# Gram products of a delta-rule attention: one 64x64 product per head in place of two smaller ones, and eight narrow PSUM copies in place of two wide ones

## The chip, the cores and the metric

The kernel runs on one core of a Trainium2 chip. The metric is the device time of one execution in microseconds: the median of the runs of a kernel. One execution of each kernel is also recorded by the hardware profiler, and the profile and trace quoted here are of that execution. Engines are named as in the profile: PE is TensorE, PEld its weight loads, DVE is VectorE, ACT is ScalarE, POOL is GpSimd, SP is SyncE, which issues the DMAs.

## The reference

Attention by a delta rule over 32 heads (4 batches of 8), 768 steps, 48 dimensions a head, and then a dense layer with softplus over the 3072 tokens (384 to 2048 to 384), all in fp32:

```python
k_n = k / (np.linalg.norm(k, axis=-1, keepdims=True) + 1e-06)
for t in range(S):
    y[:, :, t] = np.einsum('bhd,bhde->bhe', q[:, :, t], state)
    v_old = np.einsum('bhde,bhd->bhe', state, kt)
    state = state + bt[:, :, :, None] * np.einsum('bhd,bhe->bhde', kt, vt - v_old)
...
h = x @ w_in
g = np.maximum(h, 0.0) + np.log1p(np.exp(-np.abs(h)))
return g @ w_out
```

## The kernel before

The 768 steps are cut into 12 chunks of C = 64. Inside a chunk the recurrence is solved as a triangular system: for each head the matrix K K^T of the chunk (64x64, here called its Gram) is formed, its strict lower triangle is scaled and I + L is inverted by halves of HB = 32: the two 32x32 diagonal blocks are inverted on VectorE (`invert`), and the block below the diagonal is joined by products on TensorE (`cross_a`, `cross_b`). So three of the four 32x32 blocks of a Gram are needed: both diagonal ones and the one below.

The 32 heads lie in 16 pairs; a pair fills 128 partitions with 64 steps each. The keys of a chunk lie transposed in `kts[s % 3]`: 48 dimensions on the partitions, the first head of a pair in one half of them and the second in the other. `quads` (L59) lists the 32 products of a chunk so that neighbours go through all four combinations of the half that is read (`dr[ab]`) and the half of PSUM that is written (`t`). Even and odd pairs go to two PSUM tiles `pas[0]`, `pas[1]`, each 128 x 8 x 64.

`gram(s)` (L120) makes the Gram of chunks 2 to 11. First 32 products of 32x32 put the upper diagonal block at columns HB to C of the lower-numbered rows `lo` (L127), then 32 products of 32x64 put the block below the diagonal and the lower diagonal block into rows `hi` (L131). Both diagonal blocks then lie in the same columns, and one copy of 128 partitions for each parity takes them to `LTD` (`copy_diagonals`, L113, the tile is named `work`); four copies of 32 partitions take the blocks below to `OFF` (`copy_below`, L118). Chunks 0 and 1 are made by `gram_diagonal` and `gram_below` (L140, L148), of their own.

Every fp32 product is two matmul records and two weight loads in the trace. The small products write to the PSUM pool `ps_a` (tiles `pa`), which has 4 buffers that are handed out in turn: a Gram takes two, then `k_state` (L294) two, the two halves of `p_half` (L304) one each, and so on.

The order of the work: the attention of a chunk and the dense layer of an earlier chunk are generators that the loop at L720 advances in turn by a counted rate. For even s, `chunk(s)` makes the Grams of chunks s + 2 and s + 3 at its end (L556, L559), so they come in pairs close to each other: (4, 5), (6, 7), (8, 9), (10, 11); chunk 2's is in the hand-ordered start and chunk 3's stands alone. After the second Gram of a pair come the next chunk's `k_state` and `p_half`. The dense layer's products are L465 (into `ph`, waiting for softplus on ScalarE L469 to L471 and VectorE L473 to L476) and L448 (into `po`). A scheduler sets the order of each engine's queue from this program; within a queue the engine works in order. In the first chunk the weights are also rounded by a chain on VectorE (L394 to L406) with copies on ScalarE (L384, L409).

Of the kernel before, what the change touches and what calls it, by code (L numbers as in the profile page):

```python
# [20 lines left out]
C = 64  # L21
HB = 32
NS = S // C
NP = B * H // 2
# [11 lines left out]
def deltanet_moe(ctx, tc, kT, qT, kN, kI, vN, beta, wts, out):  # L36
    nc = tc.nc
# [14 lines left out]
    tk = [slice(h * C, (h + 1) * C) for h in range(2)]  # L52
    lo = [slice(h * C, h * C + HB) for h in range(2)]
    hi = [slice(h * C + HB, (h + 1) * C) for h in range(2)]
    dr = [slice((1 - h) * C, (1 - h) * C + D) for h in range(2)]
# [3 lines left out]
    quads = [(i, e, 2 * i + e, ab, ab ^ e) for i in range(NP // 2) for e in range(2)  # L59
             for ab in range(2)]  # L60
# [12 lines left out]
    W, HF, ST, OFF, TT, LTD, LDS, NN, NV, X = {}, {}, {}, {}, {}, {}, {}, {}, {}, {}  # L73
# [28 lines left out]
    def parity(t):  # L102
        return t.rearrange("p (a e) c -> p e a c", e=2)
# [3 lines left out]

        LTD[u] = one.tile([P, 2 * NP, HB], F32, name="work")

    def copy_diagonals(s, pas, c0):  # L110
        u, j = divmod(s, 2)
        for e in range(2):
            nc.scalar.copy(parity(LTD[u][:, j * NP:(j + 1) * NP])[:, e], pas[e][:, :, c0:c0 + HB])  # L113

    def copy_below(s, pas):
        for e in range(2):
            for h in range(2):
                nc.scalar.copy(parity(OFF[s])[hi[h], e], pas[e][hi[h], :, 0:HB])  # L118

    def gram(s):  # L120
        if s not in OFF:
            OFF[s] = two.tile([P, NP, HB], F32, name="off", bufs=3)
        pas = [ps_a.tile([P, NP // 2, C], F32, name="pa") for e in range(2)]
        kt = kts[s % 3]
        for i, e, p, ab, t in quads:
            k = kt[dr[ab], p, :]
            nc.tensor.matmul(pas[e][lo[t], i, HB:C], k[:, 0:HB], k[:, 0:HB],  # L127
                             start=True, stop=True)
        for i, e, p, ab, t in quads:
            k = kt[dr[ab], p, :]  # L130
            nc.tensor.matmul(pas[e][hi[t], i, :], k[:, HB:C], k, start=True, stop=True)  # L131
        copy_diagonals(s, pas, HB)
        copy_below(s, pas)

    def gram_diagonal(s, pool, name):
        pas = [pool.tile([P, NP // 2, HB], F32, name=name) for e in range(2)]
        for half in (lo, hi):
            for i, e, p, ab, t in quads:
                k = kts[s % 3][dr[ab], p, half[0].start:half[0].stop]
                nc.tensor.matmul(pas[e][half[t], i, :], k, k, start=True, stop=True)  # L140
        copy_diagonals(s, pas, 0)

    def gram_below(s):
        OFF[s] = two.tile([P, NP, HB], F32, name="off", bufs=3)
# [370 lines left out]
    def chunk(s):  # L515
# [36 lines left out]
        if more:  # L552
            u = s // 2 + 1
            systems(u)
            load_k(s + 3)
            gram(s + 2)  # L556
            cols[u] = run(nm)
            yield
            gram(s + 3)  # L559
            yield  # L560
            background.append(invert(u, *cols[u]))
# [12 lines left out]
    with tc.manual_schedule(engines={ET.PE, ET.DVE, ET.Activation, ET.Pool}):  # L574
# [28 lines left out]
        for _ in range(5):  # L603
            next(nm)
        gram_diagonal(0, ps_a, "pa")
        gram_diagonal(1, ps_a, "pa")
        cols[0] = run(nm)
        iv = invert(0, *cols[0])
# [18 lines left out]
        run(iv)  # L627
        systems(1)
        gram(2)
        finish(0)  # L630
        nm = norms(1, kas[1])
# [148 lines left out]
```

## Time and profile before

| | before |
|---|---|
| runs, us | 671.69, 673.43, 679.93 (median 673.43) |
| the profiled execution | 672.51, its span 670.8 |
| mean granted TensorE clock | 0.971 |
| matmuls of L127 and L131 | 640 records each, 9.0 and 13.2 us busy |
| copies of L113 and L118 | 24 and 48, 7.9 and 17.5 us busy |

The span is the time from the first to the last instruction of the profiled execution. A row of a timeline gives the start, the time, the engine, the line, the operation with its tiles, the shape, how many instructions are merged, and in brackets how long the engine had been idle and what released it. A row by groups gives after the bar the busy us and the mean ns of one, and the idle time before them. "issue" is time in which an engine waited for nothing that the profile shows. The idle time of an engine that others do not wait for costs nothing.

### The profile page before, as it was taken

What the parts mean: (1) busy time and instruction counts of PE and PEld (TensorE: products, weight loads), DVE (VectorE), ACT (ScalarE), POOL (GpSimd) and SP (SyncE); (2) the same over time, 40 slices, a digit from 0 to 9 for tenths busy, and PEclk for the clock granted to TensorE, in tenths of its full rate; (3) what the DMA queues carried; (4) which work ended last, traced back from release to release, by engine and by line L of the source; (5) the groups of instructions that cost most, each with busy time, mean ns of one, the idle gap of its engine ahead of it and who ended that gap; (6) DMA issues with size and microseconds to landing.
All of it is one profiled execution on the core that took longest, in us unless ns stands there. A gap on an engine that the chain in (4) does not pass through costs nothing.

```text
span 670.8 us, 24090 instructions
## 1 busy us (share of the span) xinstructions
PE 612.4 (91%) x10736; PEld 571.7 (85%) x10736; DVE 451.9 (67%) x970; ACT 372.5 (56%) x687; POOL 30.5 (5%) x56
## 2 busy tenths in 40 slices
PE   4456968899888999989999999999999999999997
PEld 3455756579888999988999999998999998999997
DVE  4966498978555985556997558985539984544443
ACT  4334767879664447464456555555554546454433
POOL 3200010000000001000001000001000001000000
PEclk9998977899998999999999999997999998999999
DMA  9837286000140120140210322200302100200000
GB/s 232 271 98 207 64 262 150 0 25 4 52 108 26 48 61 26 50 108 27 70 38 28 81 78 71 61 25 21 90 4 71 38 24 5 60 25 13 2 23 23
DMA packets 35095, 44.80 MB, mean 67 GB/s; under 512 B 21776, under 2 KB 27184, under 8 KB 34992
## 3 DMA queue, kind: packets, MB, share of 16 engines
q1 hardware_dynamic: 34992, 43.27, 22.9%
q8 instruction: 84, 1.38, 0.9%
q14 instruction: 19, 0.16, 0.1%
HBM read 36.27 MB, written 4.72 MB: 61 GB/s over the span
## 4 chain that ended last, share of the span: by engine, by line
PE 77%; ACT 8%; DVE 7%; issue 5%; DMA 2%; POOL 1%; SPq 0%; ACTq 0%; DVEq 0%; POOLq 0%
PE ph L465 29%; PE po L448 27%; PE pa L345 4%; PE pa L304 3%; PE pa L330 2%; PE pa L318 2%; PE pa L284 2%; PE pa L131 2%; PE pa L294 2%; DMA big<-qT 1%; ACT tt L275 1%; PE pa L263 1%; PE pa L127 1%; DVE ex L406 1%; DVE ex L403 1%
## 5 line engine op out<-in xcount | busy, mean ns | idle before, releaser
L465 PE MATMUL ph<-x,w 128*128 128x256 f32 x1680 | 240.9, 294 | 2.2 <-DVE a L473 0.9
L465 PEld LDWEIGHTS ph<-x,w 128*128 128x128 f32 x1680 | 224.6, 192 | 10.1 <-DVE w L419 1.2
L448 PE MATMUL po<-w,gh 128*128 128x384 f32 x768 | 208.0, 357 | 3.7 <-DVE gh L479 2.4
L469 ACT ACTIVATE a<-ph 128x512 f32<-128x512 f32 x96 | 57.5, 599 | 171.7 <-PE ph L465 171.7
L448 PEld LDWEIGHTS po<-w,gh 128*128 128x128 f32 x768 | 135.0, 190 | 13.6 <-DVE gh L479 3.2
L473 DVE SCALAR_TENSOR_TENSOR a<-ph,a 128x512 f32<-128x512 f32 x88 | 60.5, 689 | 106.6 <-ACT a L471 106.2
L448 PE MATMUL po<-w,gl 128*128 128x384 f32 x352 | 119.2, 339 | 0.0
L448 PEld LDWEIGHTS po<-w,gl 128*128 128x128 f32 x352 | 66.3, 188 | 0.5 <-DVE gl L476 0.2
L476 DVE TENSOR_TENSOR gl<-a,gh 128x512 fp32r<-128x512 f32 x88 | 60.9, 692 | 2.9
L470 ACT ACTIVATE a<-a 128x512 f32<-128x512 f32 x96 | 60.9, 634 | 2.7
L471 ACT ACTIVATE a<-a 128x512 f32<-128x512 f32 x96 | 60.8, 634 | 2.3
L229 DVE TENSOR_TENSOR Z<-Z,work 128x84 f32<-128x84 f32 (+14 forms) x148 | 44.2, 306 | 2.8
L223 DVE TENSOR_TENSOR work<-Z,ltq 128x84 f32<-128x84 f32 (+14 forms) x148 | 44.2, 305 | 2.5
L475 DVE CAST gh<-a 128x512 fp32r<-128x512 f32 x88 | 37.7, 428 | 7.7 <-PE po L448 5.6
L311 DVE TENSOR_TENSOR big<-pa,maskP 64x512 f32<-64x512 f32 x44 | 30.2, 687 | 12.9 <-PE pa L304 12.4
L345 PEld LDWEIGHTS pa<-big 128*64 128x64 f32 x768 | 27.8, 150 | 10.9 <-ACT big L322 7.1
L345 PE MATMUL pa<-big 128*64 128x64 f32 x768 | 31.0, 238 | 6.7 <-ACT big L322 5.7
L322 ACT COPY big<-pa 64x384 f32<-64x384 f32 x46 | 21.7, 473 | 19.5 <-PE pa L318 18.7
L277 POOL MEMSET tt<- 32x512 f32 x24 | 13.1, 545 | 402.3 <-PE pa L263 224.9
L304 PE MATMUL pa<-big,kt 48*64 48x64 f32 x704 | 27.4, 229 | 3.4 <-issue 2.0
L304 PEld LDWEIGHTS pa<-big,kt 48*64 48x64 f32 x704 | 24.9, 144 | 4.0 <-issue 2.3
L333 ACT COPY big<-pa 48x384 f32<-48x384 f32 x44 | 20.9, 475 | 8.4 <-PE pa L330 7.9
(103 smaller groups left out, 645.1 us busy)
## 6 DMA issues: line engine op xcount, KB each, us to landing
w<-wts SPq DMA_DIRECT2D x16, 768.0 KB, 5.6
kt<-kT SPq DMA_DIRECT2D x24, 192.0 KB, 4.3
big<-qT SPq DMA_DIRECT2D x24, 192.0 KB, 4.1
nv<-vN SPq DMA_DIRECT2D x12, 384.0 KB, 4.2
ki<-kI SPq DMA_DIRECT2D x24, 192.0 KB, 3.6
out<-ex SPq DMA_DIRECT2D x24, 192.0 KB, 1.9
ka<-kN SPq DMA_DIRECT2D x8, 384.0 KB, 3.6
x<-x SPq DMA_DIRECT2D x66, 32.0 KB, 2.2
```

Source lines behind the costliest of these rows:

```text
L223: nc.vector.tensor_tensor(tmp[:, a:a + r, 0:j], Z[:, a + j + 1:a + n, a + j:a + j + 1].to_broadcast([P, r, j]), lq[:, a + j:a + j + 1, a:a ...
L229: nc.vector.tensor_tensor(z, z, tmp[:, a:a + r, 0:j], op=ALU.add)
L304: nc.tensor.matmul(pt[tk[ab], i, :], kts[s % 3][dr[ab], 8 * g + i, :], bv[dr[ab], ab, 8 * g + i, 0:C], start=True, stop=True)
L345: nc.tensor.matmul(py[tk[ab], i, :], big[:, at + C:at + 2 * C], big[:, at:at + C], start=True, stop=True)
L448: nc.tensor.matmul(po[:, h, 0:DM], g[b][:, f - f0, h * P:(h + 1) * P], weight(f, a, DM, DM), start=(f == 0 and i == 0), stop=end)
L465: nc.tensor.matmul(ph[:, f - f0], weight(f, a, k * P, P), xr[b][k], start=(c == 0), stop=(c == len(terms1) * NK - 1))
L469: nc.scalar.activation(a, ph, AF.Abs)
L470: nc.scalar.activation(a, a, AF.Exp, scale=-1.0)
L471: nc.scalar.activation(a, a, AF.Ln, bias=1.0)
L473: nc.vector.scalar_tensor_tensor(a, ph, 0.0, a, op0=ALU.max, op1=ALU.add)
L475: nc.vector.tensor_copy(g[0], a)
L476: softplus[0] = nc.vector.tensor_tensor(g[1], a, g[0], op=ALU.subtract)
```

## The change

The whole 64x64 Gram of a head is one product: 32 products of 64x64 replace 32 of 32x32 and 32 of 32x64. The upper diagonal block now lies in columns 0 to HB of the rows `lo` and the lower one in columns HB to C of the rows `hi`, so the diagonal blocks are copied by eight copies of 32 partitions (2 parities, 2 halves, 2 blocks; new L132), where two of 128 did it. The block above the diagonal is computed and not read. `copy_diagonals` keeps its use in `gram_diagonal` alone. Lines below L131 move by one: L158 is now L159, L248 is L249, L294 is L295, L304 is L305, L448 is L449, L465 is L466, L469 is L470.

```diff
     def copy_diagonals(s, pas):
         u, j = divmod(s, 2)
         for e in range(2):
-            nc.scalar.copy(parity(LTD[u][:, j * NP:(j + 1) * NP])[:, e], pas[e][:, :, c0:c0 + HB])
+            nc.scalar.copy(parity(LTD[u][:, j * NP:(j + 1) * NP])[:, e], pas[e][:, :, 0:HB])
...
         for i, e, p, ab, t in quads:
             k = kt[dr[ab], p, :]
-            nc.tensor.matmul(pas[e][lo[t], i, HB:C], k[:, 0:HB], k[:, 0:HB],
-                             start=True, stop=True)
-        for i, e, p, ab, t in quads:
-            k = kt[dr[ab], p, :]
-            nc.tensor.matmul(pas[e][hi[t], i, :], k[:, HB:C], k, start=True, stop=True)
-        copy_diagonals(s, pas, HB)
+            nc.tensor.matmul(pas[e][tk[t], i, :], k, k, start=True, stop=True)
+        u, j = divmod(s, 2)
+        for e in range(2):
+            for h in range(2):
+                for rows, c in ((lo[h], 0), (hi[h], HB)):
+                    nc.scalar.copy(parity(LTD[u][rows, j * NP:(j + 1) * NP])[:, e],
+                                   pas[e][rows, :, c:c + HB])
         copy_below(s, pas)
```

The scheduler also orders the queues anew. ScalarE in the start, from the copies of chunk 2's Gram to the copy in the first `join` (L248, now L249); `x_84` and `ka` are natural-layout keys that are squared for the norms. Before:

```order
L113 COPY work<-pa 128x8x32 x2
L118 COPY off<-pa 32x8x32 x4
L158 ACTIVATE x_84<-x_84 128x768
L158 ACTIVATE ka<-ka 128x768
L248 COPY x_303<-pa 128x16x16
```

Changed:

```order
L132 COPY work<-pa 32x8x32 x4
L159 ACTIVATE ka<-ka 128x768
L132 COPY work<-pa 32x8x32 x4
L118 COPY off<-pa 32x8x32 x4
L159 ACTIVATE x_84<-x_84 128x768
L249 COPY x_303<-pa 128x16x16
```

The square of `ka` moved from behind the copies into the middle of them.

TensorE at the second Gram of the pair (8, 9), from chunk 9's Gram on. Before:

```order
L127 MATMUL pa<-kt_74 32x32 x32
L131 MATMUL pa<-kt_74 32x64 x32
L294 MATMUL pa<-big,kt_75 64x48 x32
L304 MATMUL pa<-big,kt_75 64x64 x16
L465 MATMUL ph<-x_5514,w_1765 128x256 x9
L465 MATMUL ph<-x_5514,w_1770 128x256 x9
L448 MATMUL po<-w_2624,gh 128x384 x2
L448 MATMUL po<-w_2624,gl 128x384
```

Changed:

```order
L127 MATMUL pa<-kt_74 64x64 x32
L295 MATMUL pa<-big,kt_75 64x48 x32
L466 MATMUL ph<-x_5358,w_1713 128x256 x9
L466 MATMUL ph<-x_5358,w_1718 128x256 x9
L449 MATMUL po<-w_2572,gh 128x384 x2
L305 MATMUL pa<-big,kt_75 64x64 x16
L449 MATMUL po<-w_2572,gl 128x384
```

`p_half` (L304, now L305) moved behind 18 products of the dense layer's first half and two of its second. At the pair (4, 5) the 18 stand ahead of `k_state` too, at (6, 7) eleven of them do, and at (10, 11) nothing moved.

ScalarE at the pair (6, 7), from the first Gram's copies on. Before:

```order
L113 COPY work<-pa 128x8x32 x2
L118 COPY off<-pa 32x8x32 x4
L113 COPY work<-pa 128x8x32
L118 COPY off<-pa 32x8x32
L113 COPY work<-pa 128x8x32
L118 COPY off<-pa 32x8x32 x3
L469 ACTIVATE a<-ph 128x512
```

Changed:

```order
L132 COPY work<-pa 32x8x32 x8
L118 COPY off<-pa 32x8x32 x4
L132 COPY work<-pa 32x8x32 x4
L118 COPY off<-pa 32x8x32 x2
L132 COPY work<-pa 32x8x32 x4
L118 COPY off<-pa 32x8x32 x2
L470 ACTIVATE a<-ph 128x512
```

The second Gram's copies go parity by parity here, the even tile first; at the pairs (4, 5) and (8, 9) all eight diagonal ones come ahead of the four below.

More of the change, by code (lines that the diff above doesn't have):

```diff
@@ L108, in systems, with copy_diagonals @@
         LTD[u] = one.tile([P, 2 * NP, HB], F32, name="work")
-    def copy_diagonals(s, pas, c0):
+    def copy_diagonals(s, pas):
         u, j = divmod(s, 2)
         for e in range(2):
-            nc.scalar.copy(parity(LTD[u][:, j * NP:(j + 1) * NP])[:, e], pas[e][:, :, c0:c0 + HB])
+            nc.scalar.copy(parity(LTD[u][:, j * NP:(j + 1) * NP])[:, e], pas[e][:, :, 0:HB])
     def copy_below(s, pas):
@@ L140, in gram_diagonal @@
                 nc.tensor.matmul(pas[e][half[t], i, :], k, k, start=True, stop=True)
-        copy_diagonals(s, pas, 0)
+        copy_diagonals(s, pas)
     def gram_below(s):
```

## The prediction

> **What bounds the kernel now.** I read the page's shares, its chain and its DMA queues first, then the busy time by stretch, the groups by shape, and the timeline around each of the ten Gram products (K K^T of a chunk).
>
> ```profile
> span 670.8 us, 24090 instructions
> PE 612.4 (91%) x10736; PEld 571.7 (85%) x10736; DVE 451.9 (67%) x970; ACT 372.5 (56%) x687; POOL 30.5 (5%) x56
> ...
> q8 instruction: 84, 1.38, 0.9%
> ...
> PE 77%; ACT 8%; DVE 7%; issue 5%; DMA 2%; POOL 1%; SPq 0%; ACTq 0%; DVEq 0%; POOLq 0%
> ```
>
> ```profile
> 72.00:122.00 50.00, 39.92 (x615) 30.75 (x608) 42.45 (x79) 37.66 (x64) 3.94 (x6) 0.86 0.52 155
> ...
> 215.00:290.00 75.00, 75.00 (x1112) 71.91 (x1111) 56.35 (x126) 40.41 (x75) 2.23 (x4) 1.00 0.19 51
> ```
>
> The columns of the second block are the stretch, then the busy us of PE, its weight loads, DVE, ACT and POOL, the granted clock, the DMA share and GB/s. After 122 us TensorE is the bound: from 215 to 290 it never rests, so whatever it waits there is paid in full. From 72 to 122 us the weights are being converted and VectorE is the fullest (42.5 of 50). 5% of the chain is "issue": TensorE has neither work nor a wait. The instruction queue hints at why: 84 packets for 2 x 10736 TensorE instructions is one packet per 256 of them.
>
> **TensorE's part.** A Gram is now 64 products, each seen as two records, so 128 records and 128 weight loads: one whole instruction packet. Here is the last one (chunk 11), with the copies of the one before it (chunk 10).
>
> ```profile
> 488.43 0.63 ACT L113 COPY work<-pa 128x256 f32<-128x256 f32 x2
> ...
> 492.53 0.72 PE L127 MATMUL pa<-kt 48*32 48x32 f32 x62
> 492.63 0.60 ACT L469 ACTIVATE a<-ph 128x512 f32<-128x512 f32 x1 [2.05 <-PE ph L465]
> ...
> 493.09 1.09 PE L131 MATMUL pa<-kt 48*32 48x64 f32 x62
> ...
> 494.11 0.62 PE L448 MATMUL po<-w,gh 128*128 128x384 f32 x2
> 494.46 0.63 ACT L113 COPY work<-pa 128x256 f32<-128x256 f32 x2
> ...
> 495.11 1.51 ACT L118 COPY off<-pa 32x256 f32<-32x256 f32 x4
> ...
> 496.42 1.15 PE L294 MATMUL pa<-big,kt 48*64 48x48 f32 x64
> 497.39 1.11 PE L304 MATMUL pa<-big,kt 48*64 48x64 f32 x32
> ...
> 498.43 2.41 PE L465 MATMUL ph<-x,w 128*128 128x256 f32 x18
> ```
>
> The 32-wide half starts at 492.53, the 64-wide half follows from about 493.07, and the next work at 494.11: 0.54 + 1.04 = 1.58 us. The new Gram has 64 records of 48x64 on 48x64, a form that this order has not had. Bounds: L294 streams 48 columns from the same stationary tile and runs 64 records in 497.39 - 496.42 = 0.97 us. L304 has the new form exactly, but its neighbours use only two of the four row and column halves; 32 records take 498.43 - 497.39 = 1.04, so 64 would take 2.08. The Gram keeps the walk over all four halves (the list `quads`), as L131 and L294 do, so I take L131's 1.04. A Gram then costs 0.54 us less, the ten 5.4 us less (bounds: 6.1 less to 5 more). It also issues half as many instructions, which matters where TensorE waits on "issue" inside or right behind a Gram.
>
> **ScalarE's part.**
>
> ```profile
> L118 ACT COPY off<-pa 32x256 f32<-32x256 f32 x48 | 17.5, 365 | 8.0 <-PE pa L148 7.3
> ...
> L113 ACT COPY work<-pa 128x256 f32<-128x256 f32 x24 | 7.9, 371 | 8.3 <-PE pa L131 4.2 <-issue 3.5 <-PE pa L140 0.3
> ```
>
> A copy of 32 partitions costs what one of 128 does (365 against 371 ns). Worse, the two wide ones overlap (2 x 0.371 took 0.63) and the narrow ones do not (4 took 1.51, 0.378 each). So a Gram's copies go from 0.63 + 1.51 = 2.14 to 12 x 0.378 = 4.54 us: 2.4 more, 24 us over ten. ScalarE is 56% busy, so most is idle time filled; the question is who waits. The Trainium skill ("ScalarE: Activation LUTs", What ACT_TABLE_LOAD costs) says that ACTIVATEs back to back overlap by about 93 ns. The wide pair agrees, the four narrow ones do not; by that rule twelve copies would take about 3.4 us, and the waits worked out below would be about 1.1 us shorter for each Gram that they queue behind.
>
> Who waits is TensorE, for PSUM. The pool `pa` has four buffers; a Gram takes two (even, odd heads), so k_state (L294) two products later needs both of the first Gram back, and p_half (L304) the even one of the second. I walk the four pairs of Grams of the steady part, with the new order of instructions.
>
> *Chunks 10, 11* (rows above). Chunk 10's copies start at 488.43 and now end at 492.97. The softplus that waited until 492.63 begins there, so chunk 11's copies begin 0.34 later, at 494.8. The even tile is free after ten of the twelve (eight diagonal ones, two below): 494.8 + 3.78 = 498.6. TensorE, 1.1 us ahead after two shorter Grams, has k_state done at 496.3, then waits 2.3 us, and p_half ends at 499.7 instead of 498.43: **+1.3**.
>
> *Chunks 8, 9.*
>
> ```profile
> 393.93 0.63 ACT L113 COPY work<-pa 128x256 f32<-128x256 f32 x2
> ...
> 397.47 1.15 PE L294 MATMUL pa<-big,kt 48*64 48x48 f32 x64
> 397.54 0.65 ACT L113 COPY work<-pa 128x256 f32<-128x256 f32 x2 [1.46 <-PE pa L131]
> ...
> 398.99 1.15 PE L304 MATMUL pa<-big,kt 48*64 48x64 f32 x32 [0.38 <-ACT off L118]
> ...
> 402.66 0.33 PE L448 MATMUL po<-w,gl 128*128 128x384 f32 x1
> ```
>
> p_half already waits 0.38 for a copy here. Chunk 8's copies now run from 393.93 to 398.5; TensorE reaches k_state at 396.4 and waits 2.1. Then the new order puts 18 ph products and two po before p_half (to 402.0); the even tile of chunk 9 is free at 398.5 + 3.8 = 402.3, so p_half ends at 403.4. The same work ended at 402.66 before (where the third po starts): **+0.7**.
>
> *Chunks 6, 7.*
>
> ```profile
> 298.00 0.65 ACT L113 COPY work<-pa 128x256 f32<-128x256 f32 x2
> ...
> 300.69 0.75 PE L131 MATMUL pa<-kt 48*32 48x64 f32 x35 [1.69 <-issue]
> ...
> 302.96 1.02 PE L304 MATMUL pa<-big,kt 48*64 48x64 f32 x27 [0.44 <-ACT off L118]
> ...
> 307.12 0.51 PE L448 MATMUL po<-w,gh 128*128 128x384 f32 x2
> ```
>
> Two Grams in a row overran their instructions: 1.69 us of "issue". With half of them that goes. The copies: chunk 6 until 298.0 + 4.5 = 302.5, when k_state starts; then, in the new order, six copies that free the even tile at 304.8. p_half 304.8 to 305.9, seven ph to 306.7 against 307.12: **-0.4**.
>
> *Chunks 4, 5.*
>
> ```profile
> 198.27 0.63 ACT L113 COPY work<-pa 128x256 f32<-128x256 f32 x2
> ...
> 203.96 1.02 PE L304 MATMUL pa<-big,kt 48*64 48x64 f32 x26 [1.39 <-issue]
> ...
> 208.66 0.52 PE L448 MATMUL po<-w,gh 128*128 128x384 f32 x2
> ```
>
> The new order has the 18 ph ahead of k_state, and 24 copies without a break: from 198.27, the even tile of chunk 5 is free after 22, at 206.6; p_half ends at 207.65, with all done that was done at 208.66: **-1.0**.
>
> **The clock.** What these waits cost besides is seen where TensorE last rested so.
>
> ```profile
> 201.53:204.94 3.41, 1.50 (x41) 1.21 (x33) 1.02 (x2) 1.26 (x4) 0.00 (x0) 0.99 0.02 5
> 204.94:208.35 3.41, 3.41 (x17) 3.41 (x17) 1.38 (x2) 0.00 (x0) 0.00 (x0) 0.51 0.02 5
> ```
>
> After 3.41 us with TensorE busy for 1.50, the next 3.41 ran at 0.51 of the clock, which costs 1.7 us if it is all work. In the pair 6, 7 TensorE would now have about 1 us of work in 5; in 8, 9 and 10, 11 it rests 2.1 and 2.3 us, so about half of the positions of such a stretch hit. I take 1.0 for the first (part of the slow stretch is waiting) and one hit of 1.7 for the other two together: **+2.7** (0 to +5). At 4, 5 one such stretch stands before and after.
>
> **The start.**
>
> ```profile
> 33.11 0.85 ACT L158 ACTIVATE ka<-ka 128x768 f32<-128x768 f32 x1 [0.48 <-DMA ka<-kN]
> 34.44 0.37 ACT L248 COPY x<-pa 128x256 f32<-128x256 f32 x1 [0.49 <-PE pa L246]
> ...
> 36.72 1.57 PE L253 MATMUL pa<-x,tt 32*32 32x16 f32 x100 [1.25 <-issue]
> ...
> 103.14 1.08 PE L131 MATMUL pa<-kt 48*32 48x64 f32 x31 [3.06 <-issue]
> ```
>
> In the new order the square of `ka`, which waits for its load until 33.11, stands between chunk 2's copies. Eight copies (3.0) and another square (0.85) come behind it, so L248's copy starts at 37.8, 3.4 late, and with it L253. Of that about 1.9 is cover, since L253 waited for instructions until 36.72 and now would have them: **+1.5**. The half packet saved should give back some 0.9 of the issue waits up to 65 us: **-0.9**. Chunk 3's Gram loses its 3.06 us of "issue", but it stands where the conversion on VectorE sets the pace, and ScalarE, which feeds it, gets 2.4 us more: **0** (-3 to +2).
>
> **Sum:** 1.3 + 0.7 - 0.4 - 1.0 + 2.7 + 1.5 - 0.9 + 0 = **+3.9 us**. The shorter Grams are in it, spent on waits. The profiled execution took 672.5 (1.7 outside its span), 0.9 under the median of 673.4; I put the median of the new kernel between 676.4 and 677.3: **677**.
>
> **Rivals.** *The gain gets through* (0.22). If the waits for copies are as short as the present 0.4 us, or the slack before the next softplus takes them, there remain 5.4 us of shorter Grams and the issue waits of 3.06, 1.69 and 1.39: 11.5 in all, 662 us. For it: the scheduler put other products before k_state at two pairs. Against it: the copies of a pair are one queue of 9 us, and 2 us of other work cannot fill it. *Issue waits stay* (0.08): if they are not about how many instructions there are, the 3.06, 1.69 and 1.39 return in some form, of which the forecast counts the last two and the 0.9 at the start as gone: +4, 681. The Trainium skill ("Runtime: NRT & Kernel Launch", Instruction fetch mechanics) holds that crossing such a 256-instruction block is mostly hidden, so that these stalls would have another cause; the packets of 256 and stalls only in runs of small products speak against it here. *The copies become the bound* (0.20), on the slower side: ScalarE's copies of a pair hold k_state and p_half, each wait of over 2 us brings a half-clock stretch, and the slow clock then also falls on full work. Five places at 1.7 (8.5) with waits as worked out (0.6) and the start at its full 3.4: +12.5, 686 us. It decides once the copies of both Grams last over 2 us longer than what stands before p_half. The Trainium skill ("TensorEngine Tiling (Array Packing)", PSUM Bottleneck) warns of just this: faster products do not empty PSUM faster; the 0.38 and 0.44 waits for L118 agree.
>
> **How the numbers follow.** Forecast 0.50, the three rivals as above. The range is **667 to 686**: from two thirds of the way to the first rival to the end of the slower one. 2%, or 13.5 us, is about what a measurement can tell from no change: below 660 needs more than the whole first rival (0.03), above 687 more than the whole third (0.06), so 0.91 for no change.
>
> **What would show it.** Grams of 1.0 to 1.1 us on TensorE, twelve ScalarE copies at 0.378, "issue" inside Grams gone, and new TensorE waits named L118 or the diagonal copy before L294 and L304, 1 to 3 us each at the four pairs, with half-clock stretches behind two or more. A Gram of 2 us, or waits under 0.5 us there, would make me wrong, as would L248's copy before 36 us.

## The result, and the profile after

The changed kernel took 683.19 us (median of 4 runs, 681.29 to 685.22) against 673.97 us for the kernel before (median of 4, 671.69 to 679.93). The ratio of the runs is 1.0101, 95% interval 1.0057 to 1.0145; that of the two medians is 1.0137. It is slower by about 1%, inside the range of the prediction and 6 us above its value. The profiled execution took 681.29 us, a span of 679.6, 8.8 more than before, at a mean granted clock of 0.965 (before 0.971). It is the shortest of the four.

The page of the changed kernel:

```profile
span 679.6 us, 22869 instructions
PE 615.5 (91%) x10096; PEld 573.8 (84%) x10096; DVE 453.6 (67%) x970; ACT 393.9 (58%) x747; POOL 30.4 (4%) x56
...
q8 instruction: 79, 1.29, 0.8%
...
PE 65%; ACT 15%; DVE 11%; DMA 5%; issue 3%; SPq 1%; ACTq 0%; DVEq 0%
```

The instructions fell as the diff says, 640 records on TensorE fewer and 60 copies more. On the chain that ended last, TensorE fell from 77% to 65% and ScalarE rose from 8% to 15%; "issue" went from 5% to 3%. TensorE's busy time nevertheless rose from 612.4 to 615.5 us, though it had fewer products: more of its work ran at half clock.

Three groups of the changed kernel:

```profile
L132 ACT COPY work<-pa 32x256 f32<-32x256 f32 x80 | 28.9, 362 | 3.3 <-issue 2.4
L305 PE MATMUL pa<-big,kt 48*64 48x64 f32 x704 | 28.0, 235 | 4.2 <-ACT off L118 4.2
L295 PE MATMUL pa<-big,kt 48*64 48x48 f32 x704 | 18.0, 236 | 3.7 <-ACT off L118 3.2 <-issue 0.5
```

TensorE now waits 3.2 + 4.2 = 7.4 us for a Gram's copies (L118) before k_state and p_half. Before, those two lines waited 0.0 and 1.3 us for them. The steady part's pair of chunks 10, 11, TensorE and ScalarE:

```profile
496.25 2.97 ACT L132 COPY work<-pa 32x256 f32<-32x256 f32 x8
...
499.23 1.50 ACT L118 COPY off<-pa 32x256 f32<-32x256 f32 x4
499.85 1.16 PE L127 MATMUL pa<-kt 48*64 48x64 f32 x64
500.75 0.60 ACT L470 ACTIVATE a<-ph 128x512 f32<-128x512 f32 x1
500.94 0.62 PE L449 MATMUL po<-w,gh 128*128 128x384 f32 x2
...
502.59 2.97 ACT L132 COPY work<-pa 32x256 f32<-32x256 f32 x8
...
503.25 1.15 PE L295 MATMUL pa<-big,kt 48*64 48x48 f32 x64
505.56 1.50 ACT L118 COPY off<-pa 32x256 f32<-32x256 f32 x4
506.36 1.93 PE L305 MATMUL pa<-big,kt 48*64 48x64 f32 x32 [1.96 <-ACT off L118]
508.21 3.12 PE L466 MATMUL ph<-x,w 128*128 128x256 f32 x18
```

Read from the top: a Gram takes 500.94 - 499.85 = 1.09 us on TensorE (1.58 before). Its twelve copies take 2.97 + 1.50 us and start when the twelve before and a softplus are done. p_half gets the even tile of chunk 11 when two of the four L118 are through, at 506.36, having waited 1.96; and then it runs in 1.93 us instead of 1.11, because the clock has fallen. The windows around these waits (columns as in the prediction, the granted clock behind POOL):

```profile
301.68:305.10 3.42, 1.69 (x21) 1.36 (x19) 0.81 (x2) 3.29 (x10) 0.00 (x0) 0.99 0.17 63
305.10:308.51 3.41, 3.09 (x80) 2.93 (x82) 1.02 (x2) 3.29 (x10) 0.00 (x0) 0.50 0.02 5
...
400.67:404.08 3.41, 1.97 (x112) 1.71 (x102) 0.00 (x0) 3.28 (x10) 0.00 (x0) 0.99 0.02 5
404.08:407.50 3.42, 3.42 (x23) 3.33 (x18) 1.02 (x2) 3.30 (x10) 0.00 (x0) 0.51 0.00 0
...
503.07:506.48 3.41, 1.45 (x70) 1.15 (x69) 2.38 (x5) 3.29 (x10) 0.00 (x0) 0.99 0.00 0
506.48:509.89 3.41, 3.41 (x40) 3.29 (x41) 1.38 (x2) 0.57 (x2) 0.00 (x0) 0.50 0.00 0
```

Three times TensorE is busy for 1.5 to 2.0 of 3.41 us while ScalarE copies without a break (3.3 of 3.41), and each time the next 3.41 us run at half clock, nearly full of work. Such a stretch costs 1.7 us when it is full of work, half its length. From 190 us on there are nine of them; before there were four (one that begins in the last 2 us is not counted).

How long TensorE was busy does not decide this by itself. In the changed kernel a stretch with 1.56 us of work was followed by full clock, and in the kernel before one with 3.15 us was followed by half clock. The two in the changed kernel, then the two in the one before:

```profile
113.91:117.32 3.41, 1.56 (x6) 0.93 (x6) 2.77 (x6) 3.41 (x6) 0.00 (x0) 1.00 0.00 0
117.32:120.73 3.41, 3.41 (x16) 2.62 (x15) 3.41 (x6) 3.31 (x6) 0.00 (x0) 1.00 0.00 0
```

```profile
556.48:559.89 3.41, 3.15 (x131) 2.85 (x127) 0.00 (x0) 2.98 (x6) 1.43 (x3) 1.00 0.02 5
559.89:563.30 3.41, 3.41 (x114) 3.41 (x106) 2.30 (x4) 0.25 (x1) 0.00 (x0) 0.50 0.02 5
```

So a long wait goes with a stretch at half clock at these three places, and the rule behind it stays open.

**Where the time went.** The start of each CAST of `gh` (88 in a run, one for each softplus, always in the same order) is a milestone that both kernels pass. In the views of that one line, before and after:

```profile
L475 DVE CAST gh<-a x88: 361/427/600, 142.7 to 663.3; 128x512 fp32r<-128x512 f32 x88
```

```profile
L476 DVE CAST gh<-a x88: 364/427/603, 141.9 to 672.1; 128x512 fp32r<-128x512 f32 x88
```

The first comes 0.8 us earlier than before, the last 8.8 later. The table gives this shift against the kernel before, in us, behind each place of the program, for all the kernels of this study (profiled executions); away from these places it hardly moves.

| behind | before at | change | 1 | 2 | 3 | 3 again | 4 | 5 | 6 |
|---|---|---|---|---|---|---|---|---|---|
| the start | 142.7 | -0.8 | -4.0 | +5.2 | -3.2 | -3.3 | +0.7 | +0.3 | -0.4 |
| Grams 4, 5 | 253.5 | +2.9 | -5.1 | +9.5 | -4.0 | -4.3 | +2.5 | +2.0 | +1.8 |
| Grams 6, 7 | 350.0 | +4.6 | -7.3 | +13.3 | -7.7 | -7.9 | +5.9 | +3.3 | +5.1 |
| Grams 8, 9 | 440.7 | +6.4 | -8.5 | +14.2 | -9.7 | -10.0 | +9.7 | +5.1 | +11.3 |
| the chunk from 465 us | 489.3 | +7.8 | -6.9 | +14.1 | -9.9 | -7.2 | +9.6 | +2.6 | +11.3 |
| Grams 10, 11 | 532.1 | +10.5 | -7.9 | +15.3 | -10.8 | -8.2 | +9.3 | +3.8 | +12.5 |
| the last | 663.3 | +8.8 | -7.8 | +15.4 | -11.5 | -9.3 | +8.3 | +2.4 | +12.6 |
| waits for a Gram's copies at k_state and p_half (1.3 before) | | 7.4 | 1.6 | 6.0 | 0.6 | 0.2 | 8.0 | 6.9 | 8.3 |
| half-clock stretches after 190 us (4 before) | | 9 | 7 | 10 | 4 | 6 | 9 | 5 | 10 |

The kernels are numbered as the experiments below. The waits are sums over the two groups of products, like the rows above.

Each kernel has its own order of the queues, so at most places a comparison mixes the edit with a new order. In 1 and 3 k_state and p_half stand at the four pairs where they stood before; in 2, 4, 5 and 6 TensorE's order differs from the change's at some pairs. At 10, 11 it is the same in all of them, except for the products that 5 and 6 add. There the place costs +2.7 us in the change, where p_half waits 1.96 us and a half-clock stretch follows. It costs about -1.0 in 1 and 3 with no such wait, -0.3 in 4 with a wait of 0.47, and +1.2 in 2, 5 and 6 with waits of 0.99 to 1.04 (5 and 6 have 1.7 us of added work in it). No half-clock stretch follows in any of these. This is the cleanest sign that the copies hold TensorE, and that the clock fell there behind the longest wait only.

### The profile page after: what moved, and what is told of

The parts are those of the page before. It is cut to its first block, busy times and chain, and to the rows that moved or that the text cites. A ratio compares the mean times of both kernels' runs of the same rounds, so it can differ in the third digit from the quotient of the medians.

```text
span 679.6 us, 22869 instructions
## 1 busy us (share of the span) xinstructions
PE 615.5 (91%) x10096; PEld 573.8 (84%) x10096; DVE 453.6 (67%) x970; ACT 393.9 (58%) x747; POOL 30.4 (4%) x56
## 4 chain that ended last, share of the span: by engine, by line
PE 65%; ACT 15%; DVE 11%; DMA 5%; issue 3%; SPq 1%; ACTq 0%; DVEq 0%
PE ph L466 26%; PE po L449 24%; PE pa L346 4%; PE pa L305 3%; ACT work L132 3%; DMA ka<-kN 3%; PE pa L319 2%; PE pa L285 2%; PE pa L331 2%; DMA w<-wts 2%; ACT off L118 2%; ACT a L472 2%; PE pa L295 1%; ACT a L471 1%; ACT tt L276 1%
## 5 line engine op out<-in xcount | busy, mean ns | idle before, releaser
L466 PE MATMUL ph<-x,w 128*128 128x256 f32 x1680 | 243.0, 296 | 4.3 <-DVE a L474 3.1
L466 PEld LDWEIGHTS ph<-x,w 128*128 128x128 f32 x1680 | 227.1, 195 | 11.8 <-DVE a L474 2.4
L449 PE MATMUL po<-w,gh 128*128 128x384 f32 x768 | 209.9, 359 | 6.7 <-DVE gh L480 6.0
L449 PEld LDWEIGHTS po<-w,gh 128*128 128x128 f32 x768 | 136.1, 191 | 17.8 <-DVE gh L480 7.6
L470 ACT ACTIVATE a<-ph 128x512 f32<-128x512 f32 x96 | 57.4, 598 | 161.3 <-PE ph L466 154.8
L474 DVE SCALAR_TENSOR_TENSOR a<-ph,a 128x512 f32<-128x512 f32 x88 | 60.6, 690 | 112.7 <-ACT a L472 112.5
L449 PE MATMUL po<-w,gl 128*128 128x384 f32 x352 | 119.8, 340 | 0.0
L449 PEld LDWEIGHTS po<-w,gl 128*128 128x128 f32 x352 | 66.7, 190 | 0.8 <-DVE gl L477 0.4
L312 DVE TENSOR_TENSOR big<-pa,maskP 64x512 f32<-64x512 f32 x44 | 30.2, 687 | 16.7 <-PE pa L305 16.2
L346 PE MATMUL pa<-big 128*64 128x64 f32 x768 | 29.6, 234 | 4.7 <-ACT big L323 4.1
L305 PE MATMUL pa<-big,kt 48*64 48x64 f32 x704 | 28.0, 235 | 4.2 <-ACT off L118 4.2
L132 ACT COPY work<-pa 32x256 f32<-32x256 f32 x80 | 28.9, 362 | 3.3 <-issue 2.4
L305 PEld LDWEIGHTS pa<-big,kt 48*64 48x64 f32 x704 | 25.4, 149 | 5.1 <-ACT off L118 4.6
```

The lines of the kernel that those rows point to most:

```text
L132: nc.scalar.copy(parity(LTD[u][rows, j * NP:(j + 1) * NP])[:, e], pas[e][rows, :, c:c + HB])
L305: nc.tensor.matmul(pt[tk[ab], i, :], kts[s % 3][dr[ab], 8 * g + i, :], bv[dr[ab], ab, 8 * g + i, 0:C], start=True, stop=True)
L346: nc.tensor.matmul(py[tk[ab], i, :], big[:, at + C:at + 2 * C], big[:, at:at + C], start=True, stop=True)
L449: nc.tensor.matmul(po[:, h, 0:DM], g[b][:, f - f0, h * P:(h + 1) * P], weight(f, a, DM, DM), start=(f == 0 and i == 0), stop=end)
L466: nc.tensor.matmul(ph[:, f - f0], weight(f, a, k * P, P), xr[b][k], start=(c == 0), stop=(c == len(terms1) * NK - 1))
L470: nc.scalar.activation(a, ph, AF.Abs)
```

## The experiments

The theory: the 64x64 products are a gain, and the copies take it away, because twelve narrow ones last 4.5 us, and k_state and p_half need a pair's PSUM tiles back before they are through; the waits then also bring half-clock stretches. Rivals: the products bring nothing; the copies cost nothing by themselves; it is the order in which the tiles come back; the clock falls for another reason.

### 1. The products alone

```diff
             nc.tensor.matmul(pas[e][tk[t], i, :], k, k, start=True, stop=True)
-        u, j = divmod(s, 2)
-        for e in range(2):
-            for h in range(2):
-                for rows, c in ((lo[h], 0), (hi[h], HB)):
-                    nc.scalar.copy(...)
+        copy_diagonals(s, pas)
         copy_below(s, pas)
```

> The 64x64 products with the two wide diagonal copies of before (the lower diagonal block is then not the right one; that part of the computation is left out). Theory (the copies' queue on ScalarE holds TensorE, and the rests bring half-clock stretches): the products alone are a gain, 0.49 us for each of ten Grams and part of the issue waits at chunks 3, 4-5 and 6-7: 5 to 10 us faster than before, 664 to 669. Rival (the 64x64 form, or the order that it brings, is what costs): 5 to 9 us slower, as the change.

Measured: 665.28 us (4 runs, 662.94 to 668.04; before on the same chip 674.96), ratio 0.9836 [0.9771, 0.9901]. The products are a gain of about 1.6%, as the theory expected, and L118's waits are down to 1.6 us. With the wide copies the scheduler also keeps k_state and p_half where they stood before, so what the narrow copies cost includes the order that comes with them. Against the change (span 662.9 against 679.6, 16.7 less) four items count: 3.2 at the start, 5.8 of L118 waits, two half-clock stretches fewer (3.4), and 2.1 of a wait for VectorE told below. That is 14.5 of the 16.7. In the start the copy of L248 comes at 35.91 us here, still 1.5 later than before: with wide copies too the square of `ka` stands among them.

### 2. The copies alone

The kernel before with its two sets of smaller products, and eight narrow copies in place of the two wide ones:

```diff
-        copy_diagonals(s, pas, HB)
+        u, j = divmod(s, 2)
+        for e in range(2):
+            for h in range(2):
+                for rows in (lo[h], hi[h]):
+                    nc.scalar.copy(parity(LTD[u][rows, j * NP:(j + 1) * NP])[:, e],
+                                   pas[e][rows, :, HB:C])
```

> The products of before with eight narrow diagonal copies in place of two. Theory (queue of copies): slower than before by 4 to 9 us, with waits of TensorE for L118 or the diagonal copies at the four pairs of Grams and more half-clock stretches after 190 us than the 4 of before. Rival (the products cost): within 2 us of before.

Measured: 686.46 us (685.52 to 687.88), ratio 1.0149 [1.0087, 1.0212]: a loss of 11.5 us where 4 to 9 were expected. The direction held and the size did not: the narrow copies cost more than the sum of the waits that I could name (6.0 us at k_state and p_half). 5.2 us of the loss are there before 143 us, where my walk over the pairs does not reach; about 2 of them come with chunk 2's copies, behind which the copy of L248 starts at 36.63 instead of 34.44. There are six half-clock stretches more than before. The order of TensorE moves here too: 15 ph products stand ahead of k_state at 6, 7 and 16 ahead of p_half at 8, 9, so a new order comes with the narrow copies even when the products are the old ones. The issue waits stay in part with the small products, 2.0 us at chunks 5 and 7, but the 3.06 us at chunk 3 are gone here as well. The Gram of chunk 7 and the wait behind it:

```profile
309.91 0.75 PE L131 MATMUL pa<-kt 48*32 48x64 f32 x36 [1.39 <-issue]
...
316.90 1.40 PE L309 MATMUL pa<-big,kt 48*64 48x64 f32 x32 [1.71 <-ACT off L118]
```

### 3. The products with wide copies

The products of the change; ScalarE copies whole columns of 128 partitions, four copies a Gram, and GpSimd moves the two blocks that then lie in the wrong tile, from SBUF to SBUF:

```diff
+        ltd = LTD[u][:, j * NP:(j + 1) * NP]
         for e in range(2):
-            for h in range(2):
-                for rows, c in ((lo[h], 0), (hi[h], HB)):
-                    nc.scalar.copy(parity(LTD[u][rows, j * NP:(j + 1) * NP])[:, e],
-                                   pas[e][rows, :, c:c + HB])
-        copy_below(s, pas)
+            nc.scalar.copy(parity(OFF[s])[:, e], pas[e][:, :, 0:HB])
+            nc.scalar.copy(parity(ltd)[:, e], pas[e][:, :, HB:C])
+        for h in range(2):
+            nc.gpsimd.tensor_copy(ltd[lo[h]], OFF[s][lo[h]])
```

> The 64x64 products, emptied by four wide copies on ScalarE (columns 0 to 32 of each parity to the tile off, which holds the block below and the upper diagonal one; columns 32 to 64 to the tile work), and the upper diagonal blocks carried from off to work by two copies of 32 partitions on the idle GpSimd. Theory (queue of copies): ScalarE's copies of a Gram fall from 4.5 to about 1.3 us, less than the 2.1 of before, so no wait of TensorE for them: 5 to 10 us faster than before, 664 to 669. Rival (the products cost): 5 to 9 us slower than before. A third: GpSimd's copies come late or slow VectorE: between the two, with waits that name GpSimd.

Measured: 660.79 us (657.19 to 660.98), ratio 0.9750 [0.9676, 0.9825], better than expected and faster than both kernels. ScalarE's copies of chunk 10 and GpSimd's behind them:

```profile
484.12 0.35 ACT L131 COPY off<-pa 128x256 f32<-128x256 f32 x1
484.37 0.38 ACT L132 COPY work<-pa 128x256 f32<-128x256 f32 x1
484.63 0.39 ACT L131 COPY off<-pa 128x256 f32<-128x256 f32 x1
484.90 0.40 ACT L132 COPY work<-pa 128x256 f32<-128x256 f32 x1
```

```profile
485.35 1.62 POOL L134 COPY work<-off 32x512 f32<-32x512 f32 x2 [3.92 <-ACT work L132]
```

Four wide copies start 0.26 us apart and free both PSUM tiles in 1.2 us, where the twelve narrow ones need 4.5. GpSimd's 1.62 us lie behind the freeing of PSUM and nothing in PSUM waits for them; no wait of TensorE in this profile names GpSimd. The waits at k_state and p_half shrink to 0.6 us. So the change lost by the form of its copies, with the order that comes with it.

The same kernel again, on another chip and with more rounds:

> The kernel with 64x64 products, four wide ScalarE copies and two GpSimd copies a Gram once more, with more rounds. If its gain of 2.5% over the kernel before is the products' and not a disturbance: 657 to 663 us and a ratio of 0.970 to 0.983.

Measured: 661.76 us (658.92 to 668.80), ratio 0.9825 [0.9774, 0.9877] against a before of 675.58. The gain stands at 1.8 to 2.5%. The two profiles of this one kernel agree to 0.3 us up to 440 us; then one has two half-clock stretches from 450 us on and the other four, and they end 2.2 us apart. What the clock does at one place is worth that much from run to run.

### 4. The even tile first

The change, with the even tile's six copies ahead of the odd one's:

```diff
                     nc.scalar.copy(parity(LTD[u][rows, j * NP:(j + 1) * NP])[:, e],
                                    pas[e][rows, :, c:c + HB])
-        copy_below(s, pas)
+            for h in range(2):
+                nc.scalar.copy(parity(OFF[s])[hi[h], e], pas[e][hi[h], :, 0:HB])
```

> The change with its twelve copies in another order: all six of the even heads' tile first, then the six of the odd. Theory (queue of copies): the even tile, for which p_half waits, is free four copies or 1.5 us sooner at the pairs where it waits, so 2 to 5 us faster than the change, 678 to 681; k_state, which needs both, gains nothing. Rival (the number of copies alone, or the products): within 1 us of the change.

Measured: 680.15 us (10 runs, 679.17 to 682.07), ratio 1.0065 [1.0031, 1.0098]. The median is 3.0 us below the change's, as the theory has it, but the intervals overlap and the two profiled spans are 0.5 apart (679.1 and 679.6), as the rival has it: the time decides nothing. The place where TensorE's order did not move does. At 10, 11 p_half waits 0.47 us instead of 1.96, the expected 1.5 less, no half-clock stretch follows, and the place costs 3.0 us less:

```profile
506.64 1.15 PE L306 MATMUL pa<-big,kt 48*64 48x64 f32 x32 [0.47 <-ACT off L135]
```

At 6, 7 and 8, 9 the scheduler took cover away: one ph product stands ahead of k_state instead of eleven, and none ahead of p_half instead of 18. These places cost 3.4 and 3.8 us instead of 1.7 and 1.8. Over all, p_half's waits for copies fall from 4.2 to 2.6 and k_state's rise from 3.2 to 5.4. So the order in which the tiles come back does count, and the other cost, that ScalarE needs twelve copies a Gram, stays.

### 5. Work put into two of the waits

To see what the clock takes, TensorE got something to do where it waits: two idle products ahead of chunk 9's Gram, four ahead of chunk 11's. They are overwritten by the Gram.

```diff
         kt = kts[s % 3]
+        for _ in range({9: 2, 11: 4}.get(s, 0)):
+            nc.tensor.matmul(pas[0][:, :, :], W[0][:, 0, 0:P], W[0][:, 0, 0:512],
+                             start=True, stop=True)
```

> The change, with idle work added to TensorE: two 128x512 products of a weight with itself ahead of chunk 9's Gram and four ahead of chunk 11's, written into the Gram's own PSUM tile and overwritten by it. They add about 6 x 0.43 = 2.6 us of work just ahead of the waits for L118. Theory (the loss at the pairs is the wait and, behind it, a stretch of 3.41 us at half the clock because TensorE was busy under 2 us in the stretch before): the added work lies inside the waits (1.44 us at k_state of chunk 8, 1.96 at p_half of chunk 10), the stretches at 404.08 and 506.48 run at full clock, and the span is 1.7 to 3.4 us shorter than the 679.6 of the change, though work was added. Rival A (the waits alone cost; the clock falls at these places for another reason): the stretches stay at half clock and the span is within 1 us of 679.6. Rival B (the added work is not covered): 1 to 3 us longer.

Measured: 679.53 us (12 runs, 674.88 to 681.44), ratio 1.0068 [1.0039, 1.0097], against the change's 1.0101 [1.0057, 1.0145]. The intervals overlap, so the time alone does not prove a gain; it speaks against the added work costing 1 to 3 us. The mean granted clock of the twelve runs has a median of 0.968, that of the change's four runs 0.959. The two places, in their windows:

```profile
398.90:402.31 3.41, 2.28 (x106) 1.79 (x108) 0.32 (x1) 3.28 (x10) 0.00 (x0) 0.99 0.02 5
402.31:405.72 3.41, 3.41 (x48) 3.32 (x41) 1.02 (x2) 3.29 (x10) 0.00 (x0) 0.50 0.00 0
...
497.90:501.31 3.41, 2.37 (x77) 2.00 (x77) 2.39 (x5) 3.29 (x10) 0.00 (x0) 1.00 0.00 0
501.31:504.70 3.39, 3.39 (x52) 3.32 (x50) 1.38 (x2) 0.57 (x3) 0.00 (x0) 1.00 0.02 5
```

At 10, 11 it went as the theory says: the wait fell from 1.96 to 1.04 us, the half-clock stretch is gone, and the place costs 3.8 - 2.6 = 1.2 us in the table instead of 10.5 - 7.8 = 2.7, the four added products included. At 8, 9 the two products were too few: the stretch stays, and the place costs 1.8 us as in the change, the added work being hidden in the wait. A busy time of 2.28 us was still followed by half clock and 2.37 was not, while 2.28 at the same place of experiment 6 was followed by full clock, so what exactly decides is not read off here. The profiled execution is also the fastest of its twelve (674.88), and its span of 673.2 is 6.4 below the change's. Only 1.5 of that stand at the two places. 3.9 stand at the chunk start at 465 us, which ran at full clock here, and 2.0 at Grams 4, 5; the order of every engine is the same as the change's at both, so I count these as chance.

### 6. Work put into all four

The same with four products each ahead of chunk 5's and 7's Grams as well: `{5: 4, 7: 4, 9: 2, 11: 4}`.

> The same with four added products also ahead of chunk 5's and chunk 7's Gram, 14 in all or about 6 us of added work; the scheduler then also puts k_state earlier and p_half a few products earlier or later at those two pairs, so it is a coarser test. Theory: half-clock stretches at the four pairs go from five to two or fewer, and the span is 2 to 7 us shorter than the change's 679.6. Rival A: the stretches stay, 679 to 682. Rival B: 681 to 686.

Measured: 684.77 us (6 runs, 682.23 to 687.60), ratio 1.0154 [1.0111, 1.0196]. The theory's 2 to 7 us less did not come: the time lies where rival B put it, and at the four pairs there are six half-clock stretches, not two or fewer. At 4, 5 the place costs 2.2 us instead of 3.7, but 6, 7 costs 3.3 instead of 1.7, about the 1.7 us of work added there, and 8, 9 costs 6.2 instead of 1.8, though 8, 9 has the same two added products as in experiment 5. The difference at 8, 9 is the order that the scheduler made:

```profile
402.78 0.32 PE L298 MATMUL pa<-big,kt 48*64 48x48 f32 x4 [0.69 <-ACT off L118]
403.54 1.14 PE L298 MATMUL pa<-big,kt 48*64 48x48 f32 x60 [0.45 <-ACT off L118]
407.30 1.97 PE L308 MATMUL pa<-big,kt 48*64 48x64 f32 x32 [2.62 <-ACT off L118]
409.20 4.21 PE L469 MATMUL ph<-x,w 128*128 128x256 f32 x18
```

```profile
403.95:407.36 3.41, 0.79 (x50) 0.67 (x43) 1.02 (x2) 3.29 (x10) 0.00 (x0) 0.99 0.00 0
407.36:410.77 3.41, 3.41 (x39) 3.29 (x40) 1.38 (x2) 0.64 (x2) 0.00 (x0) 0.50 0.02 5
410.77:414.18 3.41, 3.41 (x17) 3.41 (x16) 0.00 (x0) 0.71 (x2) 0.00 (x0) 0.50 0.00 0
```

p_half now stands ahead of the 18 ph products instead of behind them, so nothing covers its wait of 2.62 us, and two stretches at half clock follow. As a test of the clock this kernel is inconclusive, since the order moved with it. It does show the wait itself: without the 18 products as cover the same copies, with one half-clock stretch more, cost some 4 us more at one place.

## Why the prediction was right, and where its sizes were off

The mechanism held: TensorE's gain was eaten by ScalarE's copies through PSUM, and the clock took more. The sum of the steps was too small by 4.9 us of span (+3.9 forecast, +8.8 measured); the range was wide enough for it. Where the order of every engine is the same, Grams 4, 5 and the start at 465 us still differ by 2.0 and 3.9 us between the profiles of the change and of experiment 5, so a single row below is no finer than that:

| step | forecast | measured |
|---|---|---|
| the start, to 143 us | +1.5 - 0.9 = +0.6 | -0.8 |
| Grams 4, 5 | -1.0 | +3.7 |
| Grams 6, 7 | -0.4, clock +1.0 | +1.7 |
| Grams 8, 9 | +0.7 | +1.8 |
| chunk start at 465 us | none | +1.4 |
| Grams 10, 11 | +1.3 | +2.7 |
| clock at 8, 9 and 10, 11 together | +1.7 | in the two rows above |
| stretch of before at 560 us | none | -1.7 |

- **The Gram.** 1.09 us to the next work, 0.49 less; forecast 0.54. Taking L131's rate rather than L304's was right. "Issue" inside the steady Grams is gone, as is the 3.06 us at chunk 3, and the packets went from 84 to 79. The rival that issue waits stay is out. That the number of instructions is the reason is borne out at the pairs, where experiment 2 kept such waits with the small products; at chunk 3 it is not shown, since the wait went away there too.
- **The copies.** Twelve in 2.97 + 1.50 = 4.47 us, forecast 4.54. Eight narrow ones in 2.97 us are 0.371 each at a mean duration of 0.362: they do not overlap at all, the wide ones of experiment 3 do (0.26 apart at 0.35 to 0.40). The Trainium skill ("ScalarE: Activation LUTs", What ACT_TABLE_LOAD costs) gives an overlap of about 93 ns for ACTIVATEs back to back, measured on tiles of 128 partitions; the wide copies agree, and the 32-partition ones, for which it gives no figure, do not.
- **The waits.** At 10, 11 the walk over ScalarE was exact: seen from the same start (7.8 us later than before), it put chunk 11's copies at 494.8 + 7.8 = 502.6 and the even tile at 506.4; they came at 502.59 and 506.36, and p_half waited 1.96, forecast 2.3. At 8, 9 k_state waited 0.99 + 0.45 = 1.4 us, forecast 2.1. At 6, 7 it waited 1.40 + 0.34 and p_half 0.32.
- **The clock was the mis-sized term.** +2.7 was forecast, with half the stretches expected to hit at 8, 9 and 10, 11. Both hit, 6, 7 got two, one came behind 4, 5 and one more at 465 us, and the one at 560 us fell away: five more in all, up to 8.5 us at 1.7 each. At 10, 11 the stretch goes when TensorE's rest is shorter, by added work (experiment 5) or by an earlier tile (4), in one profiled execution each. The prediction's step from a rest to a stretch is not a rule, though: 1.56 us of work in 3.41 was followed by full clock and 3.15 by half. At 465 us the clock differs between two runs of one kernel as well (3 and 3 again), so 1.4 us of the loss there may be chance.
- **Grams 4, 5 is the step that failed.** The part that I worked out came: p_half waited 1.91 us and po behind it started at 208.09 instead of 208.66, -0.6 for a forecast of -1.0. The loss stands 11 us later, where the walk did not reach. Before, VectorE had softplus's step ahead of the inversion's (L473, L203); in the change the same step (L474) comes behind it (L204, L206):

```profile
214.93 0.66 DVE L473 SCALAR_TENSOR_TENSOR a<-ph,a 128x512 f32<-128x512 f32 x1
215.49 1.22 DVE L203 TENSOR_TENSOR ltq<-ltq,Z 128x1024 f32<-128x1024 f32 x1
```

```profile
215.72 1.23 DVE L204 TENSOR_TENSOR ltq<-ltq,Z 128x1024 f32<-128x1024 f32 x1
216.98 1.23 DVE L206 TENSOR_TENSOR Z<-ltq,cT 128x1024 f32<-128x1024 f32 x1
...
218.77 0.69 DVE L474 SCALAR_TENSOR_TENSOR a<-ph,a 128x512 f32<-128x512 f32 x1
```

```profile
219.51 0.43 PE L466 MATMUL ph<-x,w 128*128 128x256 f32 x1 [2.12 <-DVE a L474]
```

  So TensorE waited 2.12 us for VectorE, and 219.76 to 223.17 ran at half clock; by the table the place cost 3.7 us where the forecast had a gain of 1.0. In experiment 5 the order of every engine up to there is the same, but a half-clock stretch came at 207.71, on p_half, TensorE reached the place later, the wait was 0.61 us, and the place cost 1.7. So the new order on VectorE brings a loss here, and how large it is depends on where the clock falls. I had followed the order on TensorE and ScalarE, and not on VectorE.
- **The start.** L248's copy (L249 now) came at 37.10, 2.7 us late (forecast 3.4), and TensorE's line behind it ran without the stop for instructions. Either cause alone gives more than half of it: with wide copies and the new place of `ka`'s square the copy is 1.5 late (experiment 1), with narrow copies and the old place 2.2 (experiment 2). Of the 1.2 us that were lost by 60 us 0.8 were left at 88; the turn to -0.8 at 143 comes around chunk 3's Gram, whose term was 0 (-3 to +2).
- **The rivals.** The gain alone (experiment 1) is 675.0 - 665.3 = 9.7 us where I had 11.5, so the listed gain was about 2 us too large; the copies on top of it cost 9.7 + 9.2 = 18.9 us, by each kernel's own before, where the forecast had 677 - 662 = 15. "The copies become the bound" (686) comes a little nearer to the 8.8 us (it had 12.5, the forecast 3.9): its waits and stretches came at the pairs, its dear start did not. The Trainium skill's warning ("TensorEngine Tiling (Array Packing)", PSUM Bottleneck), that faster products do not empty PSUM faster, is what experiments 1 and 3 against the change show in numbers: with the same products, 665.3 and 660.8 us against 683.2.

What stays open: of the 11.5 us of experiment 2, some 3 of the 5.2 before 143 us were not traced to single waits; except at 10, 11 no run separates the narrow copies from the order that comes with them; and the rule by which a stretch falls to half clock is not known.

## What to carry to other kernels

When products get faster, price the evacuation that comes with them before anything else: the number of copies counts, not their partitions, and the term to work out is when the last copy that frees a PSUM tile ends against when TensorE comes back for it. A wait of 2 us on an engine that is otherwise full can cost up to 1.7 us more where the clock falls behind it, as at 10, 11; a layout that copies whole columns wide and lets an idle engine sort them out in SBUF kept the gain. And when a scheduler rebuilds the order, look at every engine's order near the moved waits, VectorE's too: a wait of 2.1 us came from an engine that the edit does not touch.

## What the runs showed of the hardware that I had not expected

- Copies of 32 partitions on ScalarE follow each other at their full duration (0.371 apart at 0.362), those of 128 partitions at 0.26 (durations 0.35 to 0.40). Per element, narrow copies are about six times as dear (four times fewer partitions at 1.4 times the spacing).
- TensorE need not be idle for the clock to fall, and its busy time does not decide it: 1.45, 1.69, 1.97 and even 3.15 of 3.41 us busy were each followed by 3.41 us at 0.50 or 0.51, while 1.56 and 2.37 were followed by 1.00, and 2.28 by either.
- Two profiles of one kernel agreed to 0.3 us over 440 us and then differed by 2.7 us, where one had two half-clock stretches and the other four.
